# Stage 1 of the DFT with the input as the moving operand, its result through DRAM

## The chip, the cores and the metric

The kernel runs on one core of a Trainium2 chip. The metric is the time of one execution in microseconds on the device. TensorE (PE) multiplies matrices; a matmul has a stationary operand, loaded as weights, and a moving operand that streams through. VectorE (DVE) and ScalarE (ACT) work on SBUF and PSUM, GpSimd (POOL) on SBUF; the queue of SyncE (SP) issues nearly all transfers, in order.

## The reference

For each of 8 batches, x of 3008 x 256 goes through a two-dimensional Fourier transform, of which the real part is kept. Its 24064 rows go through a feed-forward layer without biases: 256 to 2048, an activation, 2048 to 256.

```
X = np.fft.fft(np.fft.fft(x, axis=1), axis=2).real
h = x @ w_in
g = np.where(h >= 1, h, np.where(h <= -1, 0.0, (h + 1) ** 2 / 4.0))
return g @ w_out
```

## The kernel before

**The transform.** 3008 is 47 x 64, so the transform along the sequence is done in two stages, of length 47 and 64. The host sorts x so that position n stands beside position -n; the kernel adds the two (`fold_x`), which takes care of the real part, and the transform along the 256 columns is folded into `w_in` at the start (`fold_w_in`). Stage 1 of a batch comes in 8 chunks (`XC`). A chunk of x is a tile of 96 x 2 x 512 floats, 384 KB. For batches 1 to 7 GpSimd adds its halves into `y`, 96 x 512 (L131); then, four times, 128 columns of `y` are loaded as weights and the 96 x 96 matrix of cosines and sines `bm` moves (L270). In float32 each such matmul is two records in the trace. Four ScalarE copies (L280) put the result into `z`, which has 128 partitions, 24 groups of columns and 129 values in each; the last of these belongs to the Nyquist column, for which `yd`, the difference of the two halves of chunk 0 (L137), goes through a matmul of its own (L275). Stage 2 takes `z` as weights and a 128 x 128 matrix as what moves (L309), and ends in two float32r tiles `pqh` and `pql`, a high and a low half. `nyquist` makes one row, writes it to DRAM and reads it back onto all partitions (`nyb`).

**The layer.** A batch has three parts of its positions (k, 482 or 512 wide) and 16 slices of the hidden width, so 48 units. A unit is `gemm1` (6 matmuls into `uv`, L359), then VectorE's `us` and `h` (L362, L364, L365), ScalarE's two steps of the activation (L372, L373), VectorE's L374, ScalarE's high half `gh` (L375), and on GpSimd two subtractions that make the low half `gl` (L378). Four units later (`LAG`) `gemm2` takes `gh` and `gl` in 12 matmuls (L402). A product of two float32r numbers with enough digits is three matmuls: high by high, low by high, high by low.

**What sets the order.** The transform of batch b+1 is cut into pieces, one per chunk of stage 1, one for `nyquist`, six for stage 2, and these are strewn among the units of batch b by their weights (`fft_pieces` and the loop at the end). For batch 1 this begins in unit 25 of batch 0, so its pieces stand twice as close. A scheduler then orders each engine by priority as buffers come free; each engine works its instructions in that order, and so does SP's queue. Buffers: `y` has three, shared by other small tiles; `xt` four; `h` three; `uv` three banks; the transform one bank.

Of the kernel before, what the change touches and what calls it, by code (L numbers as in the profile page):

```python
# [18 lines left out]
NB, S, D, FF = 8, 3008, 256, 2048  # L21
NA, NBB, NC = 64, 47, 24
# [84 lines left out]


@with_exitstack
def fft_ffn_kernel(ctx: ExitStack, tc: tile.TileContext, x, cst, w_in, w_out, out):  # L110
    nc = tc.nc

    wts = ctx.enter_context(tc.tile_pool(name="wts", bufs=1))
# [4 lines left out]
    xt, yt, zt, nyb, pq = {}, {}, {}, {}, {}  # L118

    def load_x(b, q):  # L120
        tag, bufs = ("xt", 4) if b or q < 4 else ("gl", 4) if q < 7 else ("o", 2)
# [4 lines left out]
    def fold_x(b, q):  # L126

        t = xt.pop((b, q))
        if b or q % 2:
            y = sb.tile([96, CH], F32, tag="y", name=f"y_{b}_{q}", bufs=3)  # L130
            nc.gpsimd.tensor_tensor(y, t[:, 0], t[:, 1], op=ALU.add)  # L131
            yt[b, q] = [y]
        else:
            yt[b, q] = [t[:, 0], t[:, 1]]
        if q == 0:
            y = sb.tile([96, NA], F32, tag="yd", name=f"yd_{b}", bufs=1)
# [6 lines left out]
    cm = sb.tile([P, _OFF[7] - _OFF[3]], F32, tag="y", name="cm", bufs=3)  # L143
    mats = [[cm[:, (2 * m + h) * P : (2 * m + h + 1) * P] for h in range(2)] for m in range(2)]

    wh = [wts.tile([P, FF], F32R, name=f"wh{i}") for i in range(2)]
    wl = [wts.tile([P, FF], F32R, name=f"wl{i}") for i in range(2)]
    woh = wts.tile([P, NFT, D], F32R, name="woh")
# [109 lines left out]
    def stage1(b, q):  # L258
        for p in range(q, min(q + 2, XC)):
            if (b, p) in xt and (b, p) not in yt:  # L260
                fold_x(b, p)
        if q == 0:
            zt[b] = sb.tile([P, NC, P + 1], F32, tag="z", name=f"z_{b}", bufs=1)
        z, y = zt[b], yt[b, q]
        bank = fft_bank(b, f"s1_{b}_{q}")
        pt = bank[:, : GPC * 96].rearrange("p (i n) -> p i n", i=GPC)
        for i in range(GPC):
            for j, part in enumerate(y):
                lhs = part[:, i * P : (i + 1) * P]
                mm = nc.tensor.matmul(pt[:, i], lhs, bm[:96, :], start=(j == 0), stop=(j == len(y) - 1))  # L270
                if i == 0:
                    pinned(b, mm)
        if q == 0:
            pd = bank[:NA, GPC * 96 : GPC * 96 + 2 * NC]
            nc.tensor.matmul(pd, yt[b, "d"], bm[:96, : 2 * NC], start=True, stop=True)  # L275
        for h in range(2):
            for m in range(2):
                src = pt[h * NA : (h + 1) * NA].rearrange("p i (t m c) -> p m c (i t)", t=2, m=2)[:, m]
                dst = z[m * NA : (m + 1) * NA, :, (2 * q + h) * 8 : (2 * q + h + 1) * 8]
                nc.scalar.activation(dst, src, AF.Copy)  # L280
        if q == 0:
            for m in range(2):
                nc.scalar.activation(z[m * NA : (m + 1) * NA, :, P], pd[:, m * NC : (m + 1) * NC], AF.Copy)

    def nyquist(b):
        pt = fft_bank(b, f"ny_{b}")
        mm = nc.tensor.matmul(pt[:NC, :NA], zt[b][:, :, P], rm[:, :NA], start=True, stop=True)
        pinned(b, mm)
        t = sb.tile([NC, NA], F32, tag="ny", name=f"nyt_{b}", bufs=2)
        nc.scalar.activation(t, pt[:NC, :NA], AF.Copy)  # L290
        row = dr.tile([NC, NA], F32, tag="row", name=f"nyr_{b}", bufs=2)
        nc.sync.dma_start(row, t)
        for k in range(NCHUNK):
            t = sb.tile([P, CH], F32, tag="nyb", name=f"nyb_{b}_{k}", bufs=4)
            src = row[8 * k : 8 * k + 8].rearrange("c d -> (c d)").unsqueeze(0).to_broadcast([P, CH])
            nc.sync.dma_start(t, src)
            nyb[b, k] = t

    def stage2(b, h):
# [6 lines left out]
        pt = fft_bank(b, f"s2_{b}_{h}").rearrange("p (i n) -> p i n", i=4)  # L306
        for i in range(4):
            c = h * 4 + i
            mm = nc.tensor.matmul(pt[:, i], z[:, c, :P], rm, start=True, stop=True)  # L309
            if i == 0:  # L310
                pinned(b, mm)
        o = (h % 2) * (CH // 2)
# [139 lines left out]
    for i in range(n_units + LAG):  # L452
        run_steps(STEPS.get(i, ""))
        if i < n_units:
            b, r = divmod(i, per)
            r0 = 0 if b else FIRST_DFT
            if r == (0 if b else FIRST_LOAD) and b + 1 < NB:
# [9 lines left out]
            while pending and (change or not soon and done < total * (r + 1 - r0) / (per - r0)):  # L467
# [16 lines left out]
    return s_pos, (S - s_pos) % S  # L484


_INS = ["x", "cst", "moe_w_in", "moe_w_out"]


# [41 lines left out]
```

## Time and profile before

| | |
|---|---|
| median of 3 runs | 1764.72 us (1764.12 to 1766.73) |
| the profiled execution | 1765.38 us, its span 1763.6 us |
| TensorE busy | 1735.8 us, 98% of the span |
| VectorE, ScalarE, GpSimd busy | 82%, 76%, 68% |
| moved by transfers | 72.51 MB, mean 41 GB/s |

A row of the timeline has start and duration in us, engine, line, operation, output tile <- input tiles, shape, and in brackets the idle time ahead and what ended it. A row of the waits has the total in us, how often, and the longest. Matmuls are pipelined: the duration of one overlaps the next, so two starts are compared.

### The profile page before, as it was taken

What the parts mean: (1) busy time and instruction counts of PE and PEld (TensorE: products, weight loads), DVE (VectorE), ACT (ScalarE), POOL (GpSimd) and SP (SyncE); (2) the same over time, 40 slices, a digit from 0 to 9 for tenths busy, and PEclk for the clock granted to TensorE, in tenths of its full rate; (3) what the DMA queues carried; (4) which work ended last, traced back from release to release, by engine and by line L of the source; (5) the groups of instructions that cost most, each with busy time, mean ns of one, the idle gap of its engine ahead of it and who ended that gap; (6) DMA issues with size and microseconds to landing.
All of it is one profiled execution on the core that took longest, in us unless ns stands there. A gap on an engine that the chain in (4) does not pass through costs nothing.

```text
span 1763.6 us, 21942 instructions
## 1 busy us (share of the span) xinstructions
PE 1735.8 (98%) x7982; PEld 1420.5 (81%) x7982; DVE 1440.0 (82%) x1766; ACT 1346.3 (76%) x1580; POOL 1202.1 (68%) x838
## 2 busy tenths in 40 slices
PE   9988999999999999999999999999999999999998
PEld 6766888888888788888888888888888888888877
DVE  6999788888887888878888788878888788888887
ACT  5777877777777877777778877788778787777776
POOL 1545966776768766787667876677676766667775
PEclk9999999999999999999999999999999999999999
DMA  7013321010010100110001100011000000000000
GB/s 230 12 66 101 101 104 60 28 50 30 13 51 28 53 30 1 51 48 33 30 10 51 50 28 24 22 39 50 28 24 34 1 23 32 11 25 5 19 25 24
DMA packets 29963, 72.51 MB, mean 41 GB/s; under 512 B 2976, under 2 KB 8224, under 8 KB 29856
## 3 DMA queue, kind: packets, MB, share of 16 engines
q1 hardware_dynamic: 29568, 70.08, 12.1%
q8 instruction: 62, 1.02, 0.2%
q10 hardware_dynamic: 288, 1.05, 0.2%
q14 instruction: 45, 0.37, 0.1%
HBM read 43.31 MB, written 27.81 MB: 40 GB/s over the span
## 4 chain that ended last, share of the span: by engine, by line
PE 61%; ACT 10%; POOL 9%; issue 6%; DVE 5%; ACTq 0%; POOLq 0%; DVEq 0%
PE acc L402 38%; PE uv L359 19%; POOL gl L378 9%; DVE h L374 4%; ACT a L373 4%; ACT gh L375 3%; ACT a L372 3%; PE s L270 2%; PE s L309 2%; ACT z L280 1%; DVE o L414 0%; DVE h L365 0%; DVE h L364 0%; POOL y L131 0%; ACT o L412 0%
## 5 line engine op out<-in xcount | busy, mean ns | idle before, releaser
L378 POOL TENSOR_TENSOR gl<-h,gh 128x512 fp32r<-128x512 f32 (+1 forms) x765 | 1095.1, 1454 | 513.3 <-ACT gh L375 491.7
L374 DVE SCALAR_TENSOR_TENSOR h<-a,h 128x1024 f32<-128x1024 f32 (+1 forms) x385 | 578.0, 1502 | 219.7 <-ACT a L373 218.1
L375 ACT ACTIVATE gh<-h 128x1024 fp32r<-128x1024 f32 (+1 forms) x385 | 400.6, 1041 | 356.9 <-DVE h L374 344.2
L402 PE MATMUL acc<-gh,woh 128*128 128x512 f32 (+1 forms) x1536 | 608.3, 396 | 6.7 <-ACT gh L375 3.3
L402 PE MATMUL acc<-gl,woh 128*128 128x512 f32 (+1 forms) x1536 | 604.6, 394 | 9.1 <-POOL gl L378 9.1
L402 PE MATMUL acc<-gh,wol 128*128 128x512 f32 (+1 forms) x1536 | 596.2, 388 | 0.0
L372 ACT ACTIVATE a<-h,biases 128x1024 f32<-128x1024 f32 (+1 forms) x385 | 431.7, 1122 | 10.0 <-DVE h L365 7.7
L373 ACT ACTIVATE a<-a 128x1024 f32<-128x1024 f32 (+1 forms) x385 | 398.8, 1036 | 7.1
L402 PEld LDWEIGHTS acc<-gl,woh 128*128 128x128 f32 x1536 | 288.8, 188 | 76.4 <-POOL gl L378 16.8
L402 PEld LDWEIGHTS acc<-gh,woh 128*128 128x128 f32 x1536 | 289.3, 188 | 68.9 <-DVE o L414 5.5
L402 PEld LDWEIGHTS acc<-gh,wol 128*128 128x128 f32 x1536 | 289.5, 188 | 59.2
L364 DVE TENSOR_TENSOR h<-us,uv 128x512 f32<-128x512 f32 (+1 forms) x384 | 259.3, 675 | 67.2 <-POOL gl L378 27.3
L359 PE MATMUL uv<-pqh,wh 128*128 128x512 f32 (+1 forms) x768 | 303.7, 395 | 3.0 <-DVE us L362 2.9
L359 PE MATMUL uv<-pql,wh 128*128 128x512 f32 (+1 forms) x768 | 301.4, 392 | 0.0
L359 PE MATMUL uv<-pqh,wl 128*128 128x512 f32 (+1 forms) x768 | 299.5, 390 | 0.0
L362 DVE SCALAR_TENSOR_TENSOR us<-nyb,delta,uv 128x512 f32<-128x512 f32 (+1 forms) x384 | 278.5, 726 | 14.6 <-PE uv L359 13.8
L365 DVE TENSOR_TENSOR h<-us,uv 128x512 f32<-128x512 f32 (+1 forms) x384 | 256.0, 667 | 0.0
L359 PEld LDWEIGHTS uv<-pqh,wh 128*128 128x128 f32 x768 | 144.4, 188 | 40.9 <-DVE us L362 6.8
L359 PEld LDWEIGHTS uv<-pql,wh 128*128 128x128 f32 x768 | 144.6, 188 | 32.1
L359 PEld LDWEIGHTS uv<-pqh,wl 128*128 128x128 f32 x768 | 144.4, 188 | 30.5 <-issue 0.2
L131 POOL TENSOR_TENSOR y<-x 96x512 f32<-96x512 f32 x60 | 106.4, 1774 | 20.0 <-DMA x<-in_x_dram 8.2
L280 ACT ACTIVATE z<-s 64x192 f32<-64x192 f32 x256 | 86.6, 338 | 6.5 <-PE s L275 1.7
(54 smaller groups left out, 548.0 us busy)
## 6 DMA issues: line engine op xcount, KB each, us to landing
x<-in_x_dram SPq DMA_DIRECT2D x64, 384.0 KB, 3.3
out_dram<-o SPq DMA_DIRECT2D x30, 512.0 KB, 2.8
out_dram<-o SPq DMA_DIRECT2D x16, 482.0 KB, 3.0
nyb<-nyr SPq DMA_DIRECT2D x24, 256.0 KB, 3.4
raw<-in_moe_w_out_dram SPq DMA_DIRECT2D x8, 512.0 KB, 10.9
raw<-in_moe_w_in_dram SPq DMA_DIRECT2D x6, 512.0 KB, 4.5
part<-o SPq DMA_DIRECT2D x4, 512.0 KB, 3.2
o<-part SPq DMA_DIRECT2D x4, 512.0 KB
```

The lines of the kernel that those rows point to most:

```text
L131: nc.gpsimd.tensor_tensor(y, t[:, 0], t[:, 1], op=ALU.add)
L280: nc.scalar.activation(dst, src, AF.Copy)
L359: nc.tensor.matmul(t[:, :n], w[m][:, cols], r[:, m, :n], start=(j == 0), stop=(j == 2))
L362: nc.vector.scalar_tensor_tensor(us, nyb[b, k][:, :n], delta[:, f : f + 1], uv[0], op0=ALU.mult, op1=ALU.add)
L364: nc.vector.tensor_tensor(h[:, 0], us, uv[1], op=ALU.subtract)
L365: nc.vector.tensor_tensor(h[:, 1], us, uv[1], op=ALU.add)
L372: nc.scalar.activation(a[:, sl], h[:, sl], AF.Relu, bias=half, scale=0.5)
L373: nc.scalar.activation(a[:, sl], a[:, sl], AF.Square)
L374: nc.vector.scalar_tensor_tensor(h[:, sl], a[:, sl], 1.0, h[:, sl], op0=ALU.min, op1=ALU.max)
L375: nc.scalar.activation(gh[:, sl], h[:, sl], AF.Copy)
L378: eng.tensor_tensor(gl[:, sg], h[:, sg], gh[:, sg].bitcast(F32), op=ALU.subtract)
L402: nc.tensor.matmul(acc[:, :n], w[:, f, wc], g[:, sg], start=(first and j == 0), stop=(last and j == 2))
```

## The change

For batches 1 to 7 the roles in stage 1 are exchanged. After the sum `y` (L148) ScalarE rounds it to a float32r high half (L151) and GpSimd subtracts this from `y` for a low half (L152); both go into a tile of the `xt` tag. Three matmuls of 96 x 96 weights and 512 moving columns make a chunk (L309), with `bm` split in the same way once (`bmh`, `bml`). The result has the frequencies on its 96 partitions, where stage 2 wants the other index. So a ScalarE copy (L313) takes it to SBUF, a transfer writes it to a DRAM tile `zd` (L317), and after chunk 7 four transfers read `zd` back, in 512-byte pieces, as `z` (L326). The host orders the columns of these batches for it. The difference for the Nyquist column now comes from a small input of its own, `xd`, loaded behind chunk 7 (L320), with a piece of its own, `difference`: one matmul (L330), one copy (L332), two subtractions on GpSimd of 64 x 24 (L336). The pieces of stage 1 weigh 3 instead of 4. x is loaded two chunks ahead, not four. Small tiles share the tag `y`, `yd` of batch 0 goes to `o`. Batch 0 is computed as before.

```diff
 def fold_x(b, q):
         t = xt.pop((b, q))
-        if b or q % 2:
+        if b:
+            fold_later(b, q, t)
+            return
+        if q % 2:
...
+    def fold_later(b, q, t):
+        y = sb.tile([96, CH], F32, tag="y", name=f"y_{b}_{q}", bufs=3)
+        nc.gpsimd.tensor_tensor(y, t[:, 0], t[:, 1], op=ALU.add)
+        t = sb.tile([96, 2, CH], F32R, tag="xt", name=f"yhl_{b}_{q}", bufs=4)
+        hi, lo = t[:, 0], t[:, 1]
+        nc.scalar.activation(hi, y, AF.Copy)
+        nc.gpsimd.tensor_tensor(lo, y, hi.bitcast(F32), op=ALU.subtract)
+        yt[b, q] = [hi, lo]
...
-            zt[b] = sb.tile([P, NC, P + 1], F32, tag="z", name=f"z_{b}", bufs=1)
+            zt[b] = sb.tile([P, NC, P], F32, tag="z", name=f"z_{b}", bufs=1)
+            zc[b] = sb.tile([P, NC], F32, tag="zc", name=f"zc_{b}", bufs=1)
...
+    def stage1_later(b, q):
+        hi, lo = yt[b, q]
+        pt = fft_bank(b, f"s1_{b}_{q}")[:96]
+        for j, (w, y) in enumerate(((bmh, hi), (bml, hi), (bmh, lo))):
+            mm = nc.tensor.matmul(pt, w, y, start=(j == 0), stop=(j == 2))
+            if j == 0:
+                pinned(b, mm)
+        t = sb.tile([96, CH], F32, tag="y", name=f"zs_{b}_{q}", bufs=3)
+        nc.scalar.activation(t, pt, AF.Copy)
+        if q == 0:
+            zd[b] = dr.tile([96, NA // 2, P], F32, tag="zd", name=f"zd_{b}", bufs=2)
+        nc.sync.dma_start(zd[b][:, 4 * q : 4 * q + 4], t.rearrange("p (a g) -> p a g", g=P))
+        if q == XC - 1:
+            yt[b, "d"] = sb.tile([96, NA], F32, tag="y", name=f"yd_{b}", bufs=3)
+            nc.sync.dma_start(yt[b, "d"], xd[b])
+            zt[b] = sb.tile([P, NC, P], F32, tag="z", name=f"z_{b}", bufs=1)
+            for m in range(2):
+                for i in range(2):
+                    o = (2 * i + m) * NC
+                    dst = zt[b][m * NA + i * 32 : m * NA + i * 32 + 32]
+                    nc.sync.dma_start(dst, zd[b][o : o + NC].rearrange("c a g -> a c g"))
+
+    def difference(b):
+        pt = fft_bank(b, f"yd_{b}")[:NA, :96]
+        pinned(b, nc.tensor.matmul(pt, yt[b, "d"], bm[:96], start=True, stop=True))
+        t = sb.tile([NA, 96], F32, tag="y", name=f"yds_{b}", bufs=3)
+        nc.scalar.activation(t, pt, AF.Copy)
+        zc[b] = sb.tile([P, NC], F32, tag="zc", name=f"zc_{b}", bufs=1)
+        for m in range(2):
+            one, other = (t[:, (2 * i + m) * NC : (2 * i + m + 1) * NC] for i in range(2))
+            nc.gpsimd.tensor_tensor(zc[b][m * NA : (m + 1) * NA], one, other, op=ALU.subtract)
...
-            pieces.append((4, lambda q=q: stage1(b, q)))
+            pieces.append((3 if b else 4, lambda q=q: stage1(b, q)))
+        if b:
+            pieces.append((3, lambda: difference(b)))
...
-                for q in range(4):
+                for q in range(2):
                     load_x(b + 1, q)
...
-                k1 = n1 + 7 - len(pending)
-                if 4 <= k1 + 3 < XC:
-                    load_x(b + 1, k1 + 3)
+                k1 = n1 + 8 - len(pending)
+                if k1 + 1 < XC:
+                    load_x(b + 1, k1 + 1)
```

Three places of the order. The first is TensorE in batch 2, at chunk 4 of the transform of batch 3 (in `s1_3_4` the 3 is the batch; a unit's number stands in `uv_106` and `gh_105`). Before:

```order
L359 MATMUL uv_109_1_4745<-pqh_2_0_3501,wl1_72 128x482
L359 MATMUL uv_109_1_4745<-pql_2_0_3502,wh1_70 128x482
L270 MATMUL s1_3_4_4765<-cs_66,y_3_4_4614 128x96 x4
L402 MATMUL acc_96_0_4427<-gh_105_4606,woh_73 128x482
L402 MATMUL acc_96_0_4427<-gh_105_4606,wol_74 128x482
```

Of the change:

```order
L414 MATMUL uv_106_1_4680<-pqh_2_0_3472,wl1_74 128x482
L414 MATMUL uv_106_1_4680<-pql_2_0_3473,wh1_72 128x482
L309 MATMUL s1_3_4_4703<-yhl_3_4_4618,bmh_69 96x512
L309 MATMUL s1_3_4_4703<-yhl_3_4_4618,bml_70 96x512
L309 MATMUL s1_3_4_4703<-yhl_3_4_4618,bmh_69 96x512
L457 MATMUL acc_96_0_4476<-gh_102_4540,woh_75 128x482
```

The four float32 matmuls became three of 512 columns, and the chunk stands three units earlier; the pieces of stage 1 of this batch end behind `uv_116` (before: `uv_119`), and stage 2 begins behind `uv_122` (before: `uv_124`).

The second is GpSimd in the same stretch, from `gl_94` to `gl_99`. Before:

```order
L378 TENSOR_TENSOR gl_94_4166<-h_94_4161,gh_94_4165 128x512 x2
L131 TENSOR_TENSOR y_3_3_4499<-x_3_3_4225 96x512
L378 TENSOR_TENSOR gl_95_4200<-h_95_4195,gh_95_4199 128x512 x2
L378 TENSOR_TENSOR gl_96_4242<-h_96_4237,gh_96_4241 128x482 x2
L378 TENSOR_TENSOR gl_97_4297<-h_97_4292,gh_97_4296 128x482 x2
L378 TENSOR_TENSOR gl_98_4331<-h_98_4326,gh_98_4330 128x482 x2
L131 TENSOR_TENSOR y_3_4_4614<-x_3_4_4268 96x512
```

Of the change:

```order
L433 TENSOR_TENSOR gl_94_4204<-h_94_4200,gh_94_4204 128x512 x2
L148 TENSOR_TENSOR y_3_2_4372<-x_3_2_4302 96x512
L152 TENSOR_TENSOR yhl_3_2_4374<-y_3_2_4372,yhl_3_2_4374 96x512
L433 TENSOR_TENSOR gl_95_4238<-h_95_4234,gh_95_4238 128x512 x2
L433 TENSOR_TENSOR gl_96_4276<-h_96_4272,gh_96_4276 128x482 x2
L148 TENSOR_TENSOR y_3_3_4462<-x_3_3_4384 96x512
L152 TENSOR_TENSOR yhl_3_3_4464<-y_3_3_4462,yhl_3_3_4464 96x512
L433 TENSOR_TENSOR gl_97_4330<-h_97_4326,gh_97_4330 128x482 x2
L433 TENSOR_TENSOR gl_98_4364<-h_98_4360,gh_98_4364 128x482 x2
L148 TENSOR_TENSOR y_3_4_4616<-x_3_4_4474 96x512
L152 TENSOR_TENSOR yhl_3_4_4618<-y_3_4_4616,yhl_3_4_4618 96x512
```

Where one addition stood between two pairs of `gl`, there are now two instructions, and ScalarE's high half, which the second reads, has to come between them. Chunks 2 to 7 stand between `gl_94` and `gl_108`; of batch 1, at the end of batch 0, all eight stand between `gl_19` and `gl_32`.

The third is the place where GpSimd and ScalarE take the first two chunks of the next batch, at `gl_118`. Of the change, GpSimd:

```order
L433 TENSOR_TENSOR gl_118_5172<-h_118_5167,gh_118_5171 128x512 x2
L148 TENSOR_TENSOR y_4_0_6139<-x_4_0_6113 96x512
L148 TENSOR_TENSOR y_4_1_6144<-x_4_1_6115 96x512
L152 TENSOR_TENSOR yhl_4_0_6141<-y_4_0_6139,yhl_4_0_6141 96x512
L152 TENSOR_TENSOR yhl_4_1_6146<-y_4_1_6144,yhl_4_1_6146 96x512
L433 TENSOR_TENSOR gl_119_5206<-h_119_5201,gh_119_5205 128x512 x2
```

and ScalarE:

```order
L430 ACTIVATE gh_118_5171<-h_118_5167 128x1024
L428 ACTIVATE a_119_5204<-a_119_5204 128x1024
L343 ACTIVATE nyt_3_5249<-ny_3_5247 24x64
L151 ACTIVATE yhl_4_0_6141<-y_4_0_6139 96x512
L151 ACTIVATE yhl_4_1_6146<-y_4_1_6144 96x512
L430 ACTIVATE gh_119_5205<-h_119_5201 128x1024
```

Before, the additions of these chunks stood apart, `y_4_0` ahead of `gl_111`, `y_4_1` ahead of `gl_115`; now four GpSimd instructions stand in a run, and on ScalarE `gh_119` stands behind both high halves.

More of the change, by code (lines that the diff above doesn't have):

```diff
@@ L109, in fft_ffn_kernel @@
 @with_exitstack
-def fft_ffn_kernel(ctx: ExitStack, tc: tile.TileContext, x, cst, w_in, w_out, out):
+def fft_ffn_kernel(ctx: ExitStack, tc: tile.TileContext, x, xd, cst, w_in, w_out, out):
     nc = tc.nc
@@ L285, in nyquist @@
     def nyquist(b):
         pt = fft_bank(b, f"ny_{b}")
-        mm = nc.tensor.matmul(pt[:NC, :NA], zt[b][:, :, P], rm[:, :NA], start=True, stop=True)
+        mm = nc.tensor.matmul(pt[:NC, :NA], zc[b], rm[:, :NA], start=True, stop=True)
         pinned(b, mm)
-        t = sb.tile([NC, NA], F32, tag="ny", name=f"nyt_{b}", bufs=2)
+        t = sb.tile([NC, NA], F32, tag="y", name=f"nyt_{b}", bufs=3)
         nc.scalar.activation(t, pt[:NC, :NA], AF.Copy)
@@ L308, in stage2 @@
             c = h * 4 + i
-            mm = nc.tensor.matmul(pt[:, i], z[:, c, :P], rm, start=True, stop=True)
+            mm = nc.tensor.matmul(pt[:, i], z[:, c], rm, start=True, stop=True)
             if i == 0:
@@ L484, in _orders @@
     return s_pos, (S - s_pos) % S
-_INS = ["x", "cst", "moe_w_in", "moe_w_out"]
+_INS = ["x", "xd", "cst", "moe_w_in", "moe_w_out"]
 def kernel(x, moe_w_in, moe_w_out):
```

21 lines of the change are left out of this document (17 added, 4 removed).

## The prediction

> **What bounds the kernel now.** I read the busy times first, then who waited for whom, then groups by shape, then single rows in order of time.
>
> ```profile
> span 1763.6 us, 21942 instructions
> PE 1735.8 (98%) x7982; PEld 1420.5 (81%) x7982; DVE 1440.0 (82%) x1766; ACT 1346.3 (76%) x1580; POOL 1202.1 (68%) x838
> ...
> PE   9988999999999999999999999999999999999998
> ```
>
> TensorE is busy 98% of the span. Two stretches of the view of waits, TensorE alone, from 150 to 225 us (the end of batch 0) and from 225 to 1426 us (batches 1 to 6), and busy times of two stretches of 60 us (TensorE, its weight loads, VectorE, ScalarE, GpSimd):
>
> ```profile
> PE acc L402 <- POOL gl L378: 2.6, 4, 1.4
> PE s L270 <- ACT z L280: 1.5, 2, 1.1
> PE acc L402 <- ACT gh L375: 1.2, 1, 1.2
> ...
> PE acc L402 <- DVE o L414: 1.1, 4, 0.3
> ...
> 160.00:220.00 60.00, 54.57 (x263) 44.06 (x263) 47.27 (x60) 50.37 (x72) 49.19 (x35) 1.00 0.36 107
> 220.00:280.00 60.00, 59.89 (x291) 49.19 (x289) 52.52 (x65) 44.03 (x49) 37.67 (x27) 1.00 0.26 89
> ```
>
> The fourth row is all that TensorE waits in 1200 us: from 225 us on, time is taken off only by taking it off TensorE, if nothing else comes to wait. Batch 0 differs: of 160 to 220 us TensorE is idle 5.4 us, mostly for `gl`.
>
> **What the change takes from TensorE.** A chunk of stage 1 in order of time, and one with the difference column (L275):
>
> ```profile
> 719.73 0.38 PE L359 MATMUL uv<-pql,wh 128*128 128x482 f32 x1
> 719.94 1.03 PE L270 MATMUL s<-cs,y 96*128 96x96 f32 x8
> 720.75 0.47 PE L402 MATMUL acc<-gh,woh 128*128 128x482 f32 x1
> 721.06 0.38 PE L402 MATMUL acc<-gh,wol 128*128 128x482 f32 x1
> ...
> 702.17 1.03 PE L270 MATMUL s<-cs,y 96*128 96x96 f32 x8
> 703.13 0.32 PE L275 MATMUL s<-cs,yd 96*64 96x48 f32 x2
> 703.38 0.51 PE L402 MATMUL acc<-gh,woh 128*128 128x512 f32 x1
> 703.72 0.40 PE L402 MATMUL acc<-gh,wol 128*128 128x512 f32 x1
> 703.96 0.40 PE L402 MATMUL acc<-gl,woh 128*128 128x512 f32 x1
> ```
>
> Matmuls overlap, so I count from start to start. The chunk holds TensorE from 719.94 to 720.75, 0.81 us, and the first matmul behind it takes 0.31 until the next start, where its kind takes 0.22 (719.73 to 719.94 is 0.21): 0.90 us. Now a chunk is three float32r matmuls of 512 columns. The pace of that form is 703.72 to 703.96, 0.23 to 0.24 us, so 0.70; that only 96 rows and 96 columns of the array are used should change nothing in the streaming (bounds: 0.64 at the pace of 482 columns, 0.79 if the 0.09 behind the chunk stays). Gain 0.20 us (0.11 to 0.26) in 56 chunks: **11.2 us** (6 to 15). The chunk with L275 costs 703.38 - 702.17 + 0.10 = 1.31, so L275 0.41; its successor L329 is also two records, with 96 columns instead of 48 and a change of form of its own: 0.2 to 0.45. I take 0 for the seven. Stage 2 and batch 0's stage 1 keep their matmuls.
>
> **What it adds elsewhere.** Groups by shape, with the spread of one from the view by line:
>
> ```profile
> L131 POOL TENSOR_TENSOR y<-x 96x512 f32<-96x512 f32 x60 | 106.4, 1774 | 20.0 <-DMA x<-in_x_dram 8.2 <-issue 7.5 <-PE s L270 3.5
> L131 POOL TENSOR_TENSOR y<-x x60: 1260/1917/2300, 9.8 to 1398.0; 96x512 f32<-96x512 f32 x60
> L280 ACT ACTIVATE z<-s 64x192 f32<-64x192 f32 x256 | 86.6, 338 | 6.5 <-PE s L275 1.7 <-PE s L270 1.0
> L412 ACT ACTIVATE o<-acc 128x512 f32<-128x512 f32 x32 | 18.6, 581 | 3.6 <-PE acc L402 3.5
> x<-in_x_dram SPq DMA_DIRECT2D x64, 384.0 KB, 3.3
> nyb<-nyr SPq DMA_DIRECT2D x24, 256.0 KB, 3.4
> ```
>
> ScalarE loses four L280 per chunk (1.35 us) and gets two copies of 512 columns, high half and eviction, at 0.58 each by L412: 0.2 us less. VectorE gets nothing per chunk. GpSimd gets a second pass over 96x512 per chunk, the low half (L152), at 1.26 to 2.30 us as L131: 56 of them, 71 to 129 us, so 68% busy becomes 72 to 76%. And the fold is now three steps on two engines: sum on GpSimd, high half on ScalarE, low half on GpSimd. In the order the low half stands right behind its sum, ahead of the next two `gl`, so GpSimd also waits there for ScalarE, some 0.65 us.
>
> The way through DRAM: each chunk's 192 KB out, then 1.5 MB back in four transfers. By the two landing rows the write is below 3.4 us, and the load lies between 3.3 (four 384 KB transfers at once) and 13.2 (one after the other). From the last chunk's matmuls (behind `uv_116`) to the first of stage 2 (behind `uv_122`) lie six units; one unit is 18 matmuls of 0.22 to 0.23, over 4 us, so 24 us. With eviction, write and load at 20 at the most, it is hidden. `difference` needs only the 24 KB of `xd`, queued ahead of it. On SP the load waits for the last write, some 3 us; behind it stand `nyr` and the next x loads, which are due units later. I cost all of this at nothing; without that cover it would be the excess over 24 us, seven times.
>
> **Whether GpSimd's new work shows** decides the result. How late `gl` may be, near 540 us, where folds stand (GpSimd, then TensorE's matmul that reads the second half of that pair), and what the second pass meets near 670 us:
>
> ```profile
> 536.90 1.30 POOL L131 TENSOR_TENSOR y<-x 96x512 f32<-96x512 f32 x1
> 538.16 3.41 POOL L378 TENSOR_TENSOR gl<-h,gh 128x482 fp32r<-128x482 f32 x2
> 543.65 0.39 PE L402 MATMUL acc<-gl,woh 128*128 128x482 f32 x1
> ...
> 668.83 3.51 POOL L378 TENSOR_TENSOR gl<-h,gh 128x512 fp32r<-128x512 f32 x2 [2.34 <-ACT gh L375]
> 669.73 1.47 DVE L374 SCALAR_TENSOR_TENSOR h<-a,h 128x1024 f32<-128x1024 f32 x1 [0.68 <-ACT a L373]
> 671.12 0.67 DVE L365 TENSOR_TENSOR h<-us,uv 128x512 f32<-128x512 f32 x1
> 672.45 1.29 POOL L378 TENSOR_TENSOR gl<-h,gh 128x512 fp32r<-128x512 f32 x1
> 672.59 0.69 DVE L364 TENSOR_TENSOR h<-us,uv 128x512 f32<-128x512 f32 x1
> ```
>
> At 538.16 the pair is done at 541.57, 2.1 us ahead of 543.65. In the new order 1.3 us of low half and about 0.65 of waiting come in between, 1.95 us: just hidden, and with a 2.3 us low half not. Why L131 and L378 have two lengths: the pair at 668.83 takes 3.51 instead of 2 x 1.29, 0.93 more, while VectorE's L374 (both operands in SBUF) runs; beside L364 (one operand in PSUM) `gl` keeps 1.29. So a unit takes 2 x 1.29 + 0.93 = 3.5 us of something that GpSimd and L374 share, of 4.2 us that TensorE takes for it: 0.7 us are free per unit, and the idle 2.34 in the row is for two. Batches 1 to 6 place six chunks' folds (2 to 7) in 14 units. Need: 6 x (1.3 + 1.3) = 15.6. Free: 14 x 0.7 + 6 x 0.70 of TensorE's own chunk time = 14. So 2 us come out of the lead, plus about 2 of a fold in flight, where the lead is 2.1 at the narrow place above, with one pass in it already. The two first folds stand as four GpSimd rows in a run ahead of `gl_119`, 5.2 us, where no other fold is near. I take 0.4 us of wait per batch, 6 x 0.4 = **+2.4** (bounds 0, if the narrow places fall between folds, and 3 per batch, 18, if ScalarE's high half also keeps its `gh` late).
>
> The Trainium skill, page "SBUF — State Buffer", section "Who interferes with whom", says that a VectorE instruction with two SBUF inputs contends with a GpSimd instruction that reads SBUF, as an exclusive lock held for the whole instruction. This speaks against the change. The trace agrees in kind (0.93 more beside L374, nothing beside L364), but its 0.93 is below L374's whole 1.47; with all of that the free time per unit would be 0.15 us, and the sum would be that of the first rival.
>
> Batch 0's end: eight chunks in about 13 units, in a stretch where TensorE already waits for `gl` and GpSimd is 49.19 of 60 us busy. Eight more passes are 10 to 18 us of work; between 220 and 280 us GpSimd has 22 us free to catch up. Bounds 0 and 12; I take **+4**.
>
> Sum: 1763.6 - 11.2 + 2.4 + 4 = 1758.8 us of span. The profiled execution took 1765.38, 1.8 above its span, and lies 0.7 above the median of 1764.72; so the median is the span plus 1.1: **1760 us**. The forecast's own range is 1756 to 1762.
>
> **Rivals.** (1) *The second pass makes GpSimd the bound where folds are dense*: `gl` late, and with it the next `h` (three buffers), from the point at which two passes and the wait between them exceed the lead of 2.1 us. At 2 us per batch and 7 in batch 0: 1763.6 - 11.2 + 12 + 7 = 1771.4, median 1773. For it: the narrow lead, the shared resource, the four rows in a run. Against: GpSimd's 2.34 us idle per two units, and only 1.1 us of waits in 1200 us now. (2) *The full gain*: nothing shows, 1763.6 - 11.2 = 1752.4, median 1753.5. For it: slack after each fold; against it: batch 0. (3) *Costs eat the gain*: the forecast with 1 us per batch and 5 in batch 0, 1763.4, median 1764.5. (4) *The load through DRAM is late*, above 24 us instead of 20: at 30 us 7 x 6 less the gain, 1795. Against it: both landing rows.
>
> **How the numbers follow.** Forecast 37%, rival 1 27%, rival 2 14%, rival 3 18%, rival 4 4%. A measurement of this kernel tells about 0.2%, 3.5 us, from no change. Faster (below 1761.2): most of the forecast and rival 2, 46%. Same: the rest of the forecast and most of rival 3, 25%. Slower: rivals 1 and 4, 29%. The range leaves out rival 4, the far end of rival 1 and the best of rival 2: 1752 to 1776.
>
> **What would show it.** Right: a chunk (L309) starts three matmuls at 0.23 us, and its successor's first interval is back at 0.23; TensorE's matmul time falls by 11 us; from 225 us on TensorE's waits for `gl` (L433) stay below 3 us; 160 to 220 us grows its idle by some 4. Wrong: TensorE waiting for `gl` or for `us` more than 1 us per batch, ScalarE's L151 waiting for L148, L429 much above 1.5 us (rival 1); TensorE waiting for the z load at L362 (rival 4); a chunk that costs more than 0.8 us (the gain itself).

## The result: 114.8 us slower

| | before | after |
|---|---|---|
| median of the runs | 1764.73 us (1764.12 to 1766.73, 4 runs) | 1879.5 us (1879.13 to 1880.07, 4 runs) |
| ratio after to before | | 1.0644 [1.063, 1.0657] |
| span of the profiled execution | 1763.6 us | 1877.6 us |
| mean granted clock of TensorE | 0.997 | 0.975 |

The forecast was 1760 us, with a range from 1752 to 1776. From the page of the profile after: its head, and TensorE's busy share and granted clock in 40 equal slices, in tenths:

```profile
span 1877.6 us, 21551 instructions
...
PE 1770.0 (94%) x7702; PEld 1416.8 (75%) x7702; DVE 1446.5 (77%) x1767; ACT 1325.9 (71%) x1462; POOL 1260.7 (67%) x901
...
PE   8888899899989999889998999988999899999998
...
PEclk8999899999999999999999999999999999999999
```

No other engine has become the bound: TensorE's share fell from 98 to 94%, GpSimd's from 68 to 67%, of a longer span. The engines now wait for each other. The view of waits after (who waited for whom, us in all, times, longest):

```profile
DVE h L429 <- ACT a L428: 303.0, 319, 4.8
ACT yhl L151 <- POOL y L148: 114.6, 46, 3.9
...
PE uv L414 <- DVE h L420: 32.1, 21, 3.0
...
POOL yhl L152 <- ACT yhl L151: 29.4, 35, 1.6
PE acc L457 <- DVE o L469: 25.5, 17, 4.3
...
PE uv L414 <- DVE us L417: 12.8, 15, 1.5
...
PE acc L457 <- POOL gl L433: 7.2, 13, 1.2
```

ScalarE stood still for 114.6 us ahead of the high half (L151), until GpSimd had made the sum (L148). TensorE, which had waited 1.1 us between 225 and 1426 us before, now waits mostly for VectorE: for `h` (L420), `us` (L417) and for an eviction that clears its bank (L469). For `gl`, the wait that the prediction watched, it waits 7.2 us in the whole span.

How the first turns into the second, at one chunk of batch 3; the timeline after (start, length, engine, line; in brackets the idle time ahead and what ended it):

```profile
768.86 0.65 DVE L420 TENSOR_TENSOR h<-us,uv 128x482 f32<-128x482 f32 x1
...
770.00 0.58 ACT L313 ACTIVATE zs<-s 96x512 f32<-96x512 f32 x1
...
770.53 2.21 POOL L148 TENSOR_TENSOR y<-x 96x512 f32<-96x512 f32 x1
...
772.77 0.63 ACT L151 ACTIVATE yhl<-y 96x512 fp32r<-96x512 f32 x1 [2.19 <-POOL y L148]
...
773.11 0.40 PE L309 MATMUL s<-yhl,bmh 96*96 96x512 f32 x1
773.31 1.08 ACT L427 ACTIVATE a<-h,biases 128x964 f32<-128x964 f32 x1
773.35 0.40 PE L309 MATMUL s<-yhl,bml 96*96 96x512 f32 x1
773.48 1.27 POOL L152 TENSOR_TENSOR yhl<-y,yhl 96x512 fp32r<-96x512 f32 x1 [0.74 <-ACT yhl L151]
773.58 0.39 PE L309 MATMUL s<-yhl,bmh 96*96 96x512 f32 x1
774.30 0.99 ACT L430 ACTIVATE gh<-h 128x964 fp32r<-128x964 f32 x1
775.19 0.99 ACT L428 ACTIVATE a<-a 128x964 f32<-128x964 f32 x1
...
776.22 1.37 DVE L429 SCALAR_TENSOR_TENSOR h<-a,h 128x964 f32<-128x964 f32 x1 [4.00 <-ACT a L428]
777.51 0.68 DVE L469 COPY o<-acc 128x512 f32<-128x512 f32 x1
...
778.25 0.77 PE L457 MATMUL acc<-gh,woh 128*128 128x482 f32 x1 [4.28 <-DVE o L469]
...
778.81 0.61 PE L457 MATMUL acc<-gh,wol 128*128 128x482 f32 x1
...
779.22 0.61 PE L457 MATMUL acc<-gl,woh 128*128 128x482 f32 x1
```

GpSimd starts the sum at 770.53. ScalarE has nothing to do from 770.58, but its next instruction is the high half, so it stands until 772.77, and L427, L430 and L428 stand behind it, although the `h` that L427 reads has been there since 769.51 (L420). VectorE is idle for 4.00 us until L428 has ended; behind its L429 stands the eviction L469, and TensorE, which needs that bank, is idle for 4.28 us. And then its matmuls of 482 columns start 0.41 us apart (778.81, 779.22), where 0.22 is usual: after the wait it runs at half its clock (the trace's record of the clock has 0.5 from 777.3 us on, for 6.83 us).

Where the loss arises can be read off the starts of the units. The table gives the start of a unit's first matmul of the second product (`acc`) in each trace, less its start in the trace before; the second and third columns are what is added in that stretch, the last is the whole difference at the last unit. Unit 48 begins batch 1, unit 336 batch 7, which folds nothing.

| us against before | start (unit 0) | rest of batch 0 (to unit 48) | batches 1 to 6 (to unit 336) | at the last unit, in all |
|---|---|---|---|---|
| after | +7.6 | +15.9 | +90.6 | +113.3 |
| copy of the sum alone | -0.9 | +6.7 | +39.6 | +46.2 |
| without low half | +7.0 | +7.3 | +42.2 | +55.9 |
| no fold | +7.7 | -3.0 | -16.1 | -12.2 |
| high half on GpSimd | +9.2 | +11.1 | +50.5 | +70.1 |
| two passes, no ScalarE | +7.0 | +8.9 | +24.6 | +39.5 |
| start mended | -0.9 | +15.4 | +90.8 | +104.2 |
| halves further away | -0.5 | +12.0 | +6.1 | +16.7 |
| ... low half on VectorE | +2.5 | +9.6 | -9.4 | +1.9 |
| ... later in batch 0 | +0.5 | +7.4 | -10.3 | -3.3 |
| ... later still | -0.1 | +11.1 | -10.0 | 0.0 |
| ... later in batch 0, one unit closer | +0.9 | +13.2 | +9.6 | +22.6 |

The rows below the first are the experiments, each by its profiled execution. In the kernel after, batches 1 to 6 lose 15 us each, batch 0 another 16, and 7.6 us are gone before unit 0 starts. That start was not priced at all. GpSimd's first instructions and TensorE's matmul that reads `yd`, before:

```profile
7.34 0.86 POOL L137 TENSOR_TENSOR yd<-x 96x64 f32<-96x64 f32 x1 [6.08 <-DMA x<-in_x_dram]
9.76 1.67 POOL L131 TENSOR_TENSOR y<-x 96x512 f32<-96x512 f32 x1 [1.56 <-DMA x<-in_x_dram]
```

```profile
11.28 0.32 PE L275 MATMUL s<-cs,yd 96*64 96x48 f32 x2
```

and after:

```profile
9.81 1.53 POOL L137 TENSOR_TENSOR y<-x 96x512 f32<-96x512 f32 x1 [8.56 <-DMA x<-in_x_dram]
13.43 1.36 POOL L137 TENSOR_TENSOR y<-x 96x512 f32<-96x512 f32 x1 [2.08 <-DMA x<-in_x_dram]
14.75 0.76 POOL L143 TENSOR_TENSOR yd<-x 96x64 f32<-96x64 f32 x1
```

```profile
15.57 0.32 PE L295 MATMUL s<-cs,yd 96*64 96x48 f32 x2 [3.97 <-POOL yd L143]
```

`yd`, the small difference that the first chunk's matmuls need, now takes its buffer from the tag `o`, and stands third instead of first on GpSimd; TensorE waits 3.97 us for it, and goes on at half clock there too (from 16.1 us on, for 10.24 us).

### The profile page after: what moved, and what is told of

Same layout as the page of the kernel before. It is cut to its first block, busy times and chain, and to the rows that moved or that the text cites. A ratio compares the mean times of both kernels' runs of the same rounds, so it can differ in the third digit from the quotient of the medians.

```text
span 1877.6 us, 21551 instructions
## 1 busy us (share of the span) xinstructions
PE 1770.0 (94%) x7702; PEld 1416.8 (75%) x7702; DVE 1446.5 (77%) x1767; ACT 1325.9 (71%) x1462; POOL 1260.7 (67%) x901
## 4 chain that ended last, share of the span: by engine, by line
PE 26%; POOL 21%; ACT 19%; issue 11%; DVE 10%; ACTq 0%; POOLq 0%; DVEq 0%
PE acc L457 17%; POOL gl L433 16%; DVE h L429 9%; PE uv L414 8%; ACT a L428 7%; ACT gh L430 6%; ACT a L427 5%; POOL y L148 4%; POOL yhl L152 1%; PE s L362 1%; DVE h L420 1%; ACT yhl L151 0%; DVE h L419 0%; DVE o L469 0%; PE s L309 0%
## 5 line engine op out<-in xcount | busy, mean ns | idle before, releaser
L433 POOL TENSOR_TENSOR gl<-h,gh 128x512 fp32r<-128x512 f32 (+1 forms) x765 | 1091.9, 1449 | 554.6 <-ACT gh L430 533.3
L429 DVE SCALAR_TENSOR_TENSOR h<-a,h 128x1024 f32<-128x1024 f32 (+1 forms) x385 | 582.7, 1514 | 304.3 <-ACT a L428 303.0
L430 ACT ACTIVATE gh<-h 128x1024 fp32r<-128x1024 f32 (+1 forms) x385 | 400.1, 1039 | 359.3 <-DVE h L429 321.1
L457 PE MATMUL acc<-gl,woh 128*128 128x512 f32 (+1 forms) x1536 | 611.3, 398 | 7.2 <-POOL gl L433 7.2
L457 PE MATMUL acc<-gh,wol 128*128 128x512 f32 (+1 forms) x1536 | 603.2, 393 | 0.0
L427 ACT ACTIVATE a<-h,biases 128x1024 f32<-128x1024 f32 (+1 forms) x385 | 431.7, 1122 | 21.0 <-DVE h L420 18.7
L428 ACT ACTIVATE a<-a 128x1024 f32<-128x1024 f32 (+1 forms) x385 | 398.5, 1035 | 6.8
L457 PEld LDWEIGHTS acc<-gh,woh 128*128 128x128 f32 x1536 | 293.9, 191 | 106.0 <-DVE o L469 33.1
L414 PE MATMUL uv<-pqh,wh 128*128 128x512 f32 (+1 forms) x768 | 310.3, 404 | 45.1 <-DVE h L420 32.1
L457 PEld LDWEIGHTS acc<-gl,woh 128*128 128x128 f32 x1536 | 293.7, 191 | 75.3 <-POOL gl L433 14.0
L457 PEld LDWEIGHTS acc<-gh,wol 128*128 128x128 f32 x1536 | 294.4, 192 | 61.7
L417 DVE SCALAR_TENSOR_TENSOR us<-nyb,delta,uv 128x512 f32<-128x512 f32 (+1 forms) x384 | 278.7, 727 | 33.2 <-PE uv L414 33.0
L420 DVE TENSOR_TENSOR h<-us,uv 128x512 f32<-128x512 f32 (+1 forms) x384 | 256.3, 667 | 0.0
L151 ACT ACTIVATE yhl<-y 96x512 fp32r<-96x512 f32 x56 | 35.3, 630 | 114.6 <-POOL y L148 114.6
L152 POOL TENSOR_TENSOR yhl<-y,yhl 96x512 fp32r<-96x512 f32 x56 | 75.9, 1360 | 33.3 <-ACT yhl L151 29.4
```

What stands on the lines that cost most here:

```text
L152: nc.gpsimd.tensor_tensor(lo, y, hi.bitcast(F32), op=ALU.subtract)
L414: nc.tensor.matmul(t[:, :n], w[m][:, cols], r[:, m, :n], start=(j == 0), stop=(j == 2))
L417: nc.vector.scalar_tensor_tensor(us, nyb[b, k][:, :n], delta[:, f : f + 1], uv[0], op0=ALU.mult, op1=ALU.add)
L420: nc.vector.tensor_tensor(h[:, 1], us, uv[1], op=ALU.add)
L427: nc.scalar.activation(a[:, sl], h[:, sl], AF.Relu, bias=half, scale=0.5)
L428: nc.scalar.activation(a[:, sl], a[:, sl], AF.Square)
```

## The experiments

The theory after the result is that of the **hand-over**: the fold now goes from GpSimd to ScalarE and back, ScalarE works in order, and its wait for a sum that GpSimd begins late stops the units behind it. The rival is that of **GpSimd's work**: the second pass itself is what is dear, since it holds GpSimd and what GpSimd shares with VectorE.

**1. The hand-over alone, in the kernel before.** One copy by ScalarE, in place, for each of the 56 chunks.

```diff
             nc.gpsimd.tensor_tensor(y, t[:, 0], t[:, 1], op=ALU.add)
+            if b:
+                nc.scalar.activation(y, y, AF.Copy)
             yt[b, q] = [y]
```

> The kernel before, and in batches 1 to 7 one ScalarE copy of the sum y onto itself (96x512) between GpSimd's sum and TensorE's matmuls: the hand-over from GpSimd to ScalarE alone, with one GpSimd pass, the float32 matmuls, no DRAM. Hand-over theory (ScalarE, working in order, stands still at the high half until GpSimd's sum is there, and holds the activation steps and gh behind it; VectorE and TensorE follow, and a long wait of TensorE halves its clock): 1764.7 plus 40 to 90 us, 1805 to 1855. GpSimd rival (the second pass and the shared port are the cause): within 4 us of 1764.7, as 56 copies of 0.6 us on ScalarE are hidden. DRAM and new-order rival (the way of z, the earlier pieces): the same, within 4 us.

Measured: 1809.45 us, ratio 1.024 [1.0188, 1.0291]. From its view of waits:

```profile
ACT y L133 <- POOL y L131: 45.2, 20, 2.9
...
PE uv L361 <- DVE h L367: 20.5, 18, 2.6
```

A copy that computes nothing new, and not on GpSimd, costs 39.6 us in batches 1 to 6. The hand-over is dear by itself, without a second pass.

**2. Without the low half.** The hand-over stays, GpSimd is back to one pass; a chunk has two matmuls instead of three.

```diff
         nc.scalar.activation(hi, y, AF.Copy)
-        nc.gpsimd.tensor_tensor(lo, y, hi.bitcast(F32), op=ALU.subtract)
-        yt[b, q] = [hi, lo]
+        yt[b, q] = [hi, None]
...
-        for j, (w, y) in enumerate(((bmh, hi), (bml, hi), (bmh, lo))):
+        for j, (w, y) in enumerate(((bmh, hi), (bml, hi))):
```

> The changed kernel without the low half of y: no L152, two matmuls per chunk instead of three (the product with the low half is left out). GpSimd is back at one pass. Hand-over theory: the waits of ScalarE for the sum stay, so 1879.5 less 56 x 0.23 = 13 us and a few more, 1840 to 1866. GpSimd rival: the loss goes, 1764.7 - 24 + 8 from the start = 1749, at most 1765. DRAM and new-order rival: 1866.

Measured: 1822.76 us, ratio 1.0315 [1.0266, 1.0365], 56.7 below the changed kernel. The matmul left out is 56 x 0.235 = 13 us of it, so some 44 us go with the second pass, and with it GpSimd's wait for the high half. ScalarE's wait moved little, from 114.6 us:

```profile
ACT yhl L151 <- POOL y L148: 97.6, 41, 3.7
```

The time lies between what the two theories expected, so neither is enough alone: the hand-over without the pass still costs, and the pass costs on top.

**3. No fold at all.** The matmuls read halves that have long been there. It serves as the floor: the new matmuls, the way through DRAM and the new order, without the fold's work on GpSimd and ScalarE.

```diff
     def fold_later(b, q, t):
-        y = sb.tile([96, CH], F32, tag="y", name=f"y_{b}_{q}", bufs=3)
...
-        yt[b, q] = [hi, lo]
+        yt[b, q] = [p[:96, 0] for p in pq[b - 1, 2]]
```

> The changed kernel with no fold at all in batches 1 to 7: the three matmuls read an older pair of float32r tiles instead, x is loaded and not used; sum, high half and low half are left out. TensorE's stream and the way through DRAM stay. Hand-over theory and GpSimd rival: 1764.7 - 11 + 8 (start) = 1762, 1755 to 1768. DRAM and new-order rival: above 1850.

Measured: 1753.53 us, ratio 0.9938 [0.9911, 0.9965], just below what both theories expected, although it starts 7.7 us late. So nothing of the loss behind the start comes from the matmuls, the DRAM way or the order of stage 2.

**4. The high half on GpSimd.** No hand-over, but three passes on GpSimd.

```diff
-        nc.scalar.activation(hi, y, AF.Copy)
+        nc.gpsimd.tensor_copy(hi, y)
```

> The changed kernel with the high half made by GpSimd instead of ScalarE: three GpSimd passes per chunk and no hand-over. Hand-over theory: the 115 us of ScalarE's waits for y go and most of the loss with them, 1765 to 1805. GpSimd rival: a third pass, 56 x 0.6 to 1.3 us, makes it slower than 1879.5, 1900 to 1960. DRAM and new-order rival: 1879.

Measured: 1835.67 us, ratio 1.0388 [1.0341, 1.0436], between what the two theories expected. From its view of waits, VectorE and TensorE:

```profile
DVE h L419 <- POOL gl L433: 77.9, 54, 5.4
PE uv L414 <- DVE h L420: 22.9, 30, 1.2
```

With three passes `h` waits for its buffer, which `gl` gives free late: the rival's mechanism does exist. TensorE's waits for `h` are shorter than in the kernel after (1.2 us at the longest, there 3.0), but there are more of them (30, there 21).

**5. Two passes, no ScalarE.** The high half is an old tile, the low half the sum less that tile.

```diff
-        nc.scalar.activation(hi, y, AF.Copy)
-        nc.gpsimd.tensor_tensor(lo, y, hi.bitcast(F32), op=ALU.subtract)
-        yt[b, q] = [hi, lo]
+        nc.gpsimd.tensor_tensor(lo, y, pq[b - 1, 2][0][:96, 0].bitcast(F32), op=ALU.subtract)
+        yt[b, q] = [pq[b - 1, 2][0][:96, 0], lo]
```

> The changed kernel, but the high half is an old tile that is long finished, and the low half is the sum less that tile: GpSimd keeps its two passes for each of 56 chunks, and ScalarE has no part in the fold (the high half is left out, so what is computed is another sum). The kernel without any fold took 1753.5 us, the changed kernel 1879.5. Hand-over theory (ScalarE, which works in order, stands still for GpSimd's sum): no wait of ScalarE for the sum is left; the second pass of about 1.36 us costs a little by itself, 1755 to 1785 us. GpSimd theory (the passes themselves make the low halves of h late): 1800 to 1835 us, with TensorE or VectorE waiting for gl. Since the kernel with the copy on GpSimd and three passes took 1835.7, something between 1753 and 1836 must come out, and the place in it divides the loss between the two.

Measured: 1805.78 us, ratio 1.0224 [1.0204, 1.0244]. This lies in the range of the rival (1800 to 1835), above that of the hand-over theory: two passes cost more than that theory allowed. In batches 1 to 6 the table has -16.1 without a fold, +24.6 with two passes, +90.6 with the hand-over besides. So of 106.7 us above the floor, 40.7 come with two passes that stand one right behind the other, and 66.0 with the hand-over added to them, the copy itself included. The split holds for this order of adding: with one pass the hand-over cost 39.6 (experiment 1), and the 40.7 depend on where the passes stand (experiment 7).

Two things about the passes show in the traces. VectorE waits for `gl` to give the buffer of the next `h` free, 50.6 us here, against 27.3 before and 11.7 without a fold:

```profile
DVE h L418 <- POOL gl L432: 50.6, 55, 3.2
```

And VectorE's L374 of the kernel before takes longer. This group without a fold (there L423), with one pass (before), with two (here L428), and in the kernel after, also with two (L429):

```profile
L423 DVE SCALAR_TENSOR_TENSOR h<-a,h 128x1024 f32<-128x1024 f32 (+1 forms) x385 | 551.7, 1433 | 169.6 <-ACT a L422 167.9
```

```profile
L374 DVE SCALAR_TENSOR_TENSOR h<-a,h 128x1024 f32<-128x1024 f32 (+1 forms) x385 | 578.0, 1502 | 219.7 <-ACT a L373 218.1
```

```profile
L428 DVE SCALAR_TENSOR_TENSOR h<-a,h 128x1024 f32<-128x1024 f32 (+1 forms) x385 | 603.7, 1568 | 208.9 <-ACT a L427 207.7
```

```profile
L429 DVE SCALAR_TENSOR_TENSOR h<-a,h 128x1024 f32<-128x1024 f32 (+1 forms) x385 | 582.7, 1514 | 304.3 <-ACT a L428 303.0
```

More passes make the group longer, but not by a fixed amount: 551.7 us without a pass; 578.0 us with one in the kernel before, but 558.1 us with one in experiment 9; 603.7 us with two here, but 582.7 us with two in the kernel after. Behind these rows: the Trainium skill, page "SBUF — State Buffer", section "Who interferes with whom", says that a VectorE instruction with two SBUF inputs contends with a GpSimd instruction that reads SBUF. The groups agree with the direction; how much a pass adds depends in these runs on more than its number.

**6. The start.** `yd` of batch 0 takes its buffer from the tag `nyb` instead of `o`.

```diff
-            y = sb.tile([96, NA], F32, tag="o", name=f"yd_{b}", bufs=2)
+            y = sb.tile([96, NA], F32, tag="nyb", name=f"yd_{b}", bufs=4)
```

> The changed kernel, but the fold of the input's last column of each batch has a tile of its own again instead of a share of the output's, as before the change. Theory of the start: GpSimd makes the first of these folds ahead of the others again, stage one of batch 0 starts some 4 us sooner, and TensorE doesn't fall to half its clock there: 7 to 8 us less, 1872 us, with unit 0 starting at the same time as before the change. Rival (the start was late for another reason, and the units catch up): within 2 us of 1879.5.

Measured: 1871.9 us, ratio 1.0598 [1.0577, 1.062]. GpSimd makes `yd` first again, and unit 0 starts 0.9 us ahead of the kernel before: the 7.6 us were the place of one small instruction in GpSimd's order.

**7. The same work, placed otherwise.** With the start mended, the two halves are queued behind the halves of an earlier unit, so that on GpSimd mostly a pair of `gl` lies between the sum and its use. (`unit` is the unit for which the chunk is called, `halves` holds each unit's L430 and L433.)

```diff
+HL, HL_FIRST = 3, (5, 4)
...
-        nc.scalar.activation(hi, y, AF.Copy)
-        nc.gpsimd.tensor_tensor(lo, y, hi.bitcast(F32), op=ALU.subtract)
+        u = unit[0] - (HL_FIRST[q] if q < 2 else HL)
+        with tc.issue_after(halves[u][0]):
+            nc.scalar.activation(hi, y, AF.Copy)
+        with tc.issue_after(halves[u][1]):
+            nc.gpsimd.tensor_tensor(lo, y, hi.bitcast(F32), op=ALU.subtract)
```

> The changed kernel with the start mended as in the kernel beside it, and with the two halves of a chunk put further from its sum in the engines' order: ScalarE's high half is queued behind the high half of the unit three earlier than the one in which the chunk is called for (five and four for a batch's first two chunks), GpSimd's low half behind that unit's low half, so that mostly a pair of gl instructions lies between the sum and its use. Same instructions, same data. Hand-over theory: ScalarE's wait for the sum falls from 114.6 us to below 20, TensorE's waits and its stretches at half clock go with it, and the time comes to 1750 to 1775 us. GpSimd theory (the second pass is what is dear, wherever it stands): 1800 to 1835 us.

Measured: 1786.11 us (1782.2 to 1786.46), ratio 1.0113 [1.0096, 1.013]: 85.8 us below the kernel of experiment 6, with the same instructions on the same engines. ScalarE's wait for the sum in experiment 6, and here, where the high half is L156 and the sum L151:

```profile
ACT yhl L151 <- POOL y L148: 114.8, 46, 3.9
```

```profile
ACT yhl L156 <- POOL y L151: 28.9, 18, 5.1
```

ScalarE's wait fell from 114.8 to 28.9 us (below 20 was expected), and the mean granted clock rose from 0.98 to between 0.991 and 0.996. ScalarE still makes its 56 copies, so their own time was not the larger part of the cost.

This moves both halves, so not all of the gain is the hand-over's. In batches 1 to 6 this kernel stands at +6.1 us, below the one of experiment 5 (+24.6), which has two passes and no hand-over at all. So of the 84.7 us that the move brings back there, at least 18.5 belong to the passes, which no longer stand one right behind the other; at most 66.2 are left for the hand-over, still the larger part. That the time stays above the forecast of the hand-over theory leaves a part to the second pass.

**8. The second pass on VectorE.** As 7, but VectorE makes the low half, behind `h` (L429 of the changed kernel) of the unit after.

```diff
-        with tc.issue_after(halves[u][1]):
-            nc.gpsimd.tensor_tensor(lo, y, hi.bitcast(F32), op=ALU.subtract)
+        with tc.issue_after(halves[u + 1][1]):
+            nc.vector.tensor_tensor(lo, y, hi.bitcast(F32), op=ALU.subtract)
```

> The kernel with the halves further from the sum (1786.1 us), but VectorE makes the low half of each chunk, queued behind the h (minimum and maximum) of the unit after the one behind whose gh the high half is queued; GpSimd keeps one pass for a chunk, as it had before the change. If the rest of that kernel's loss (it is still some 33 us above the kernel without any fold, less the start) is the second pass on GpSimd: 1752 to 1768 us, batches 1 to 6 each 1 to 3 us shorter than before the change. If it is only the longer work on whichever engine does it (VectorE is busy for 82% of the span before): 1775 to 1800 us, with TensorE waiting for h of L425 and L426.

Measured: 1767.15 us, ratio 1.0008 [0.9997, 1.0018]. Batches 1 to 6 go from +6.1 to -9.4 us: 15.5 us, by which the second pass is dearer on GpSimd than on VectorE, each in its place. (By their medians the two kernels lie 19.0 us apart; the profiled execution of experiment 7 is the fastest of its four.) What VectorE does for it:

```profile
L158 DVE TENSOR_TENSOR yhl<-y,yhl 96x512 fp32r<-96x512 f32 x56 | 51.0, 911 | 0.4 <-ACT yhl L156 0.4
```

**9. Batch 0.** As 8, with the loads and the first folds of batch 1 later in batch 0.

```diff
-FIRST_LOAD, FIRST_DFT = 21, 25
+FIRST_LOAD, FIRST_DFT = 24, 29
```

> The kernel beside it (low half on VectorE), and the first folds and the first DFT of batch 1 begin four units later within batch 0 (its loads three units later), where gl leads its use by 6 us and more instead of by 0.1 to 2. If batch 0's own loss (13.7 us between its units 24 and 48 with the halves further from the sum) comes from the narrow units 20 to 27: 4 to 10 us less than the kernel beside it. If it comes from the amount of work in batch 0's last units, which are now fewer for the same pieces: no gain, or some us more.

Measured: 1762.94 us, ratio 0.999 [0.9979, 1.0001], 4.2 us below experiment 8. By the table it is 5.2: 2.0 in the start, where nothing was changed, 2.2 in batch 0 and 0.9 later. So the units avoided here, where `gl` comes just before its use, are a small part of batch 0's loss.

**10. Later still** (26 and 32 in that line).

> The kernel that took 1762.9 us, with the first folds and the first DFT of batch 1 another three units later in batch 0 (its loads two units later). There batch 0 still lost some 7 us between its units 20 and 48, with TensorE waiting 3.3 us for VectorE's and 2.4 us for ScalarE's halves of the chunks. If the loss still comes from folds that meet narrow units: 2 to 4 us less, 1758 to 1761 us. If it comes from the pieces being crowded into batch 0's last units: 2 to 6 us more.

Measured: 1767.87 us, ratio 1.0014 [1.0005, 1.0023], 4.9 us more than experiment 9, as expected if the pieces are crowded into batch 0's last units: by the table batch 0 loses 11.1 us instead of 7.4.

**11. One unit closer.** As 9, with `HL, HL_FIRST = 2, (4, 3)`.

> The kernel that took 1762.9 us, with the halves one unit later in the engines' order (two units behind instead of three; four and three for a batch's first two chunks). ScalarE's wait for the sum, 22 us over eight places, all in batch 0 and the first chunks, should fall to a third; if these waits are what batch 0 and a batch's first chunks still lose by: 2 to 5 us less, 1758 to 1761 us. If TensorE then waits for the halves instead: the same, or 1 to 4 us more.

Measured: 1785.62 us, ratio 1.011 [1.0095, 1.0126]: 22.7 us more than experiment 9. ScalarE's wait did fall, from 22.0 to 13.2 us, but TensorE now waits for `us` (L423 here), in batches 1 to 6 nearly always (16 of 18 waits) for one that stands right behind VectorE's low half:

```profile
PE uv L420 <- DVE us L423: 13.7, 22, 1.4
...
ACT yhl L156 <- POOL y L151: 13.2, 4, 4.3
```

Again only the place sets the price, and neither expectation had it in this size. In experiment 9 the low half mostly stands right ahead of a `us` as well (39 of the 45 that the trace has in batches 1 to 6, here 44), but there it takes 801 ns on average, here 1110. Why it takes longer here was not tried.

**12. Experiment 9 in more rounds.**

> The same kernel as the one that took 1762.9 us against 1765.5 us, in more rounds, to tell whether it is below the kernel before. By the starts of the units in its profile it is 3.3 us shorter: ratio 0.998, with an interval that ends below 1. If what was seen was the spread of the runs: a ratio of 0.9995 to 1.0005.

Measured: 1763.55 us against 1767.12, ratio 0.9986 [0.9977, 0.9994]. It is faster than the kernel before, by 0.14%. Its view of waits, TensorE alone, from 310 to 1440 us (of the profile of experiment 9):

```profile
PE yd L336 <- DMA yd<-in_xd_dram: 1.2, 4, 0.3
PE acc L464 <- DVE o L476: 0.4, 1, 0.4
PE yd L336 <- ACT a L434: 0.2, 1, 0.2
```

TensorE waits for 1.8 us in 1130, nearly as little as before the change (1.1 in 1201).

## Why the prediction was wrong, point by point

**What TensorE gains: right, and it can be had.** A chunk's three matmuls start 0.24 and 0.23 us apart (773.11, 773.35, 773.58 above), as predicted. The forecast was 56 x 0.20 = 11.2 us, 1.6 for a batch; experiment 9, with no waits left, is 10.3 us shorter in batches 1 to 6, 1.7 for a batch. (Experiment 3 has 2.7; it has no fold at all, and where TensorE gains the rest was not taken apart.)

**The way through DRAM: right, it costs nothing.** No wait of TensorE for `z` is in the trace after. The transfers stayed within the bounds (us from issue to landing, last):

```profile
z<-zd SPq DMA_DIRECT2D x28, 384.0 KB, 5.8
...
zd<-zs SPq DMA_DIRECT2D x56, 192.0 KB, 2.1
```

**The failed step is the sentence "so GpSimd also waits there for ScalarE, some 0.65 us".** It saw that the fold had become three steps on two engines, and priced only the way back: GpSimd's wait for the high half, which is 29.4 us in 35 places, 0.84 each. The way out was left without a price: ScalarE waits for the sum in 46 places, 2.5 us each, 114.6 us in all. The prediction itself says that ScalarE's part of a chunk is "0.2 us less": that counts how long its instructions last, not how long they stand. For GpSimd and for SP's queue it names what stands behind a waiting instruction; for ScalarE it does not, where L427, L428 and so VectorE's L429 and the evictions stand behind L151. The order rows ahead of the prediction show this at `gl_118` ("`gh_119` stands behind both high halves"), and the bound of 18 us for `gh` named it, though as a mishap of the first chunks alone. Measured, the hand-over is 66.0 of the 106.7 us that batches 1 to 6 lose against the floor (39.6 where there is only one pass), where the prediction had 2.4 for all of the fold there.

**GpSimd's second pass was in the right place and too small.** The working found what GpSimd and L374 share, 3.5 of 4.2 us per unit, and a need that just exceeds the free time (15.6 against 14), then made of it 0.4 us for a batch. The need leaves out the wait of 0.65 us per chunk that the same working had found, 3.9 more for six chunks, and takes each pass at 1.3 us, where the sum took 1.56 and the low half 1.36 on average in the trace after. Measured, two passes one right behind the other cost 40.7 us in six batches against none, and 15.5 us go when VectorE makes the low half (experiment 8). The prediction watched `gl`, but TensorE waited for it only 7.2 us. It waited for VectorE, and VectorE for ScalarE: the idle time ahead of L429 that ScalarE's L428 ended rose from 218.1 to 303.0 us, while L429 itself took 582.7 us against 578.0.

**Batch 0** was priced at 4 with a bound of 12; it lost 15.9, 23.5 with the start. (That TensorE waits there mostly for `gl` was a loose reading: `gl` is 2.6 of the 5.3 us in the three rows shown.) **The start** is not in the sum: the prediction took it that batch 0 is computed as before, and did not ask what it means that `yd` changes its tag, and with it its place in GpSimd's order. That could be seen in the order.

**The half clock** was no term either. Of the layer's matmuls and those of L309, 157 take over 560 ns in the trace after, and 9 of the layer's before. At half clock they start 0.41 us apart instead of 0.22, so this adds up to some 30 us, against some 2 before. This is a quarter of the loss, and it follows the waits: with them it went in experiment 7, where 25 such matmuls are left in the profiled execution.

**The rivals.** Rival 1 had the sign, and ScalarE's L151 waiting for L148 was on its list of signs; its price of 2 us for a batch stands against 15.1 lost and 1.6 gained, some 17. Rival 2, the full gain, came out in batches 1 to 6 once the halves were moved and VectorE made the low one. Rival 4 did not happen. None of the cases held a loss above some 30 us, because none priced what stands behind ScalarE's wait.

What stays open: why batch 0 still loses some 7 us in experiment 9 where the others gain, how the 66.0 us of the hand-over divide between a single wait's length and the order behind it, and by which way the second pass's own part reaches TensorE. In the rows at 772.77, a wait of 2.19 and a copy of 0.54 us became 4.28 us on TensorE; the rest of that was not taken apart.

## What to carry to other kernels

When an operation moves so that a step goes from one engine to another and back, price both hand-overs, and for each engine ask what is queued behind the step that waits: a copy of 0.6 us on an engine that was a quarter idle cost 40 to 66 us in 48 uses. Compare places in the order, not only sums of busy time; moving two instructions by a few units brought 86 us back at unchanged work, part of it because two passes on one engine no longer stood one right behind the other. If a tile changes its tag or its buffers, look where its first use now stands, at the start of the kernel above all.

## What the runs showed of the hardware

**Behind waits of about 3 us TensorE's clock mostly fell to half, so that such a wait costs more than its own length.** Two waits in the trace after, with the matmuls behind them, TensorE alone:

```profile
819.82 0.49 PE L414 MATMUL uv<-pqh,wh 128*128 128x482 f32 x1 [2.94 <-DVE h L420]
820.15 0.38 PE L414 MATMUL uv<-pqh,wl 128*128 128x482 f32 x1
820.37 0.38 PE L414 MATMUL uv<-pql,wh 128*128 128x482 f32 x1
```

```profile
1047.55 0.77 PE L414 MATMUL uv<-pqh,wh 128*128 128x482 f32 x1 [2.94 <-DVE h L420]
1048.12 0.61 PE L414 MATMUL uv<-pqh,wl 128*128 128x482 f32 x1
1048.52 0.60 PE L414 MATMUL uv<-pql,wh 128*128 128x482 f32 x1
```

After the first, matmuls of 482 columns start 0.22 us apart, after the second 0.40, though both waits are 2.94 us long. Of the 14 waits of 2.9 to 4.3 us behind 150 us, 13 were followed by 4 to 14 such slow matmuls; the trace's record of the clock has 19 stretches at half ahead of the last instructions, 3.41 us long or two or three times that, where that of the kernel before has two. In batch 0 waits of 2.0 to 2.4 us did it too, where several stood close together.

The Trainium skill, page "TensorE: Matmul & The Clock Gate", section "Part 1: The HAM clock gate (the "warmup" mystery)", gives a free-running window of 4096 cycles, 3413 ns, and half clock after an idle window of about that length. The stretches agree with that length, and that the same wait does it or doesn't agrees with a free-running window; but waits of 2.94 us, shorter than the window, were enough here (3.32 us from the start of the last matmul ahead to the next start), so in this trace the limit lies below a whole idle window.
